# Tables' complex product formed by three real products, with the tables stored by quads of channels

## The chip, the cores and the metric

The kernel runs on one core of one Trainium2 chip. The metric is the device time of one execution in microseconds (us). The core has four engines that do work here: PE (TensorE, matmuls; PEld is its weight load), DVE (VectorE), ACT (ScalarE) and POOL (GpSimd); SP is the engine whose queue issues most of the DMAs. Each engine runs its own instructions strictly in the order in which they were written, and waits at an instruction until what it needs (data, or a buffer to come free) is there.

## The reference

Two branches work on one input x (2048 x 512) and are mixed by a gate:

```python
g = _sigmoid((x * gate_w).sum(-1, keepdims=True))
a = _A_ref(x, ...)      # a long convolution per channel
b = _B_ref(x, ...)      # linear attention with 32 heads
return g * a + (1 - g) * b
```

The change lies in branch A. For each of the 512 channels d it needs a convolution kernel over 2048 time steps l, the real part of a sum over 128 states n of complex exponentials:

```python
logdA = dt * A
P = jnp.exp(logdA[:, :, None] * l[None, None, :])
K = jnp.einsum("dn,dnl,dn->dl", Cc, P, dB).real
```

K is then convolved with the input through a Fourier transform, and a skip term is added.

## The kernel before, in words

**How K is built.** The time index is split in three: l = 512a + 64b + r, with a in 0..3, b in 0..7 and 64 values of r. exp(logdA * l) is then the product of a factor that depends on a (it takes Cc and dB in as well; table Ctab, complex), one that depends on b (table Dtab, complex) and one that depends on r (R, complex, cos and sin rows times a real exponential). States n lie on the 128 partitions; the sum over n is the matmul's contraction. The complex product Ctab x Dtab gives the stationary operand A: 4 x 8 = 32 columns for each channel and each part, and `kgen_chunk` (L168) multiplies it with R into the PSUM tile kps.

**Units.** The 512 channels are done in 16 units of 32. For each unit `plan_conv` writes, in this order by name: A1, A2, A3 (DVE, the product of the tables, L1113 and L1124), Rh and Rl (DVE, L1131 and L1135), kps (PE, L179), KD (its eviction from PSUM, on ACT but for the last), then the transform of two units together (psA, XA, psB, XK, t, psz, Zr, and a turn through DRAM, Zd and ZT, or on DVE). There is one buffer for A, two for R.

**The product before.** Ctab is stored as three planes o = 0, 1, 2 (minus one part, the other part, plus the first part), each of 4 x 256 channels for each half of the channels. Dtab is two planes of 8 x 512. A1 multiplies planes 0 and 1 of Ctab with plane 0 of Dtab, A2 planes 1 and 2 with plane 1; each is one DVE instruction that writes 2048 elements. What is left is the sum of both halves. A string of 16 digits, FOURS, says for each unit who adds: where it is 0 (units 2, 8, 14 and 15) a third DVE instruction A3 (L1124) adds the two halves and PE has two terms (64 matmuls); where it is 1 (the other 12 units) there is no A3, and PE adds in PSUM, with four terms (128 matmuls).

**How the tables are made.** `prepare` makes them, once for each half h of the channels, in steps named p_... on ACT and DVE, between the key stage of branch B and the first unit. ACT makes magnitudes (p_d, Exp into Dtab; p_ce into pmag) and sines and cosines (p_sn into the tile trg, which has one buffer that serves Ctab, then Dtab, then the other half). DVE multiplies: p_pr, p_px and p_cn for Ctab (L393/L394, L433, L440), p_dd and p_de for Dtab (L394, L449).

**What sets the order.** Nothing is scheduled at run time. All steps are nodes of a plan, and the long string ORDER lists the order in which they are written; the string SIDES says for some evictions whether ACT or DVE does them. Waits are derived from which instruction reads and writes which bytes, and from the rings of buffers. PSUM tiles come from rings of two or three; the steps argC (PE, args<-statC, L1035, whose result ACT turns into the sines cs) of the first four units use the same ring `ps` of two buffers as the last steps of the input's transform, psBu, whose evictions (xst, L145 on ACT, L147 on DVE) stand in the queues around the table steps. The sums of branch B's key stage (vp, its eviction vb, vr on DVE at L777, kvp on PE at L785) end at the same place.

Of the kernel before, what the change touches and what calls it, by code (L numbers as in the profile page):

```python
# [194 lines left out]
def prepare(P, nc, g, evict, psum):  # L195
# [227 lines left out]
    for h in range(2):  # L423
# [7 lines left out]
        V("p_pr", lambda h=h, hs=hs: tt(C[h][:, 2], mag()[:, :, hs], F.sc[:, 0], ALU.mult), r="s0 t7 t8", w=f"C{h}")  # L431
        V("p_pr", lambda h=h, hs=hs: tt(C[h][:, 1], mag()[:, :, hs], F.sc[:, 1], ALU.mult), r="s1 t7 t8", w=f"Ci{h}")
        V("p_cn", lambda h=h: nc.vector.tensor_scalar(out=C[h][:, 0], in0=C[h][:, 2], scalar1=-1.0, scalar2=None, op0=ALU.mult), r=f"C{h}", w=f"Cn{h}")  # L433

        def by(o, k, i, h=h, hs=hs):
            tt(o.rearrange("p k a c -> p (k a) c"), C[h][:, i:i + 2].rearrange("p k a c -> p (k a) c"), F.xy[:, k, hs].unsqueeze(1).to_broadcast([128, 8, 256]), ALU.mult)
        V("p_px", lambda by=by: by(F.P[:], 0, 1), r=f"t3 C{h} Ci{h}", w="t5 t6")
        V("p_px", lambda by=by: by(F.Q[:], 1, 0), r=f"t3 Cn{h} Ci{h}", w="t0 t1")
        V("p_px", lambda h=h: tt(C[h][:, 0:2], F.P[:], F.Q[:], ALU.add), r="t0 t1 t5 t6", w=f"Cn{h} Ci{h}")
        V("p_cn", lambda h=h: nc.vector.tensor_scalar(out=C[h][:, 2], in0=C[h][:, 0], scalar1=-1.0, scalar2=None, op0=ALU.mult), r=f"Cn{h}", w=f"C{h}")  # L440
# [631 lines left out]
def plan_conv(P, nc, g, psum, r):  # L1072
# [27 lines left out]
    def kgen(units, XA, new, split=False):  # L1100
        K = Bag()
        K.done, kps, nu = [], [], len(units)
        for cc, U in enumerate(units):
# [4 lines left out]
            d0 = 32 * U

            def half(k, c=c, d0=d0, U=U):  # L1110
                cf = g.C[U // 8][:, k:k + 2, :, d0 % 256:d0 % 256 + 32].rearrange("p o a (q l) -> p (o a) q l", l=4)
# [1 line left out]
                nc.vector.tensor_tensor(out=c.A[:, :, 64 * k:64 * k + 64, :].rearrange("p q (x b) l -> p x b q l", b=8),  # L1113
                                        in0=cf.unsqueeze(2).to_broadcast([128, 8, 8, 8, 4]), in1=df.unsqueeze(1).to_broadcast([128, 8, 8, 8, 4]), op=ALU.mult)
# [523 lines left out]
```

## Time and profile before

| what | before |
|---|---|
| median of three runs | 253.44 us (252.9, 253.44, 254.3) |
| span of the profiled execution | 252.7 us |
| PE, PEld busy | 196.8 us (78%), 132.5 us (52%) |
| DVE busy | 231.5 us (92%) |
| ACT busy | 220.4 us (87%) |
| POOL busy | 20.5 us (8%) |
| mean granted TensorE clock | 0.942 |
| DMA moved | 34.60 MB |

The span is the time from the first to the last instruction of the profiled execution, and the page has no other time of that execution; the median lies 0.74 us above it. Times within the trace are counted from the span's start. In a row of a timeline stand the start, the duration, the engine, the line, the operation, what it writes and reads, and in square brackets how long the engine sat idle before it and what ended that. Where a row has a count, its duration spans from the start of the first to the end of the last.

### The profile page before, as it was taken

The numbers are of one execution on the slowest core, as the hardware profiler recorded it, in microseconds if no ns is written. First come the engines' busy times: TensorE is split into PE (matmuls) and PEld (weight loads), VectorE is DVE, ScalarE is ACT, GpSimd is POOL, SyncE is SP. The second block draws the span as 40 slices with busy tenths as digits, with TensorE's granted clock in tenths as the row PEclk, the third lists the DMA queues.
The fourth block names the chain that finished last, engine by engine and source line by source line (L and its number), as shares of the span: only waits on it lengthen the run. The fifth ranks groups of instructions, "written<-read, shape, count | busy, mean of one in ns | idle before, by whom it ended". The sixth has DMA issues, their size and how long they took to land.

```text
span 252.7 us, 9846 instructions
## 1 busy us (share of the span) xinstructions
PE 196.8 (78%) x4386; PEld 132.5 (52%) x4386; DVE 231.5 (92%) x313; ACT 220.4 (87%) x305; POOL 20.5 (8%) x36
## 2 busy tenths in 40 slices
PE   0378899999977489799577866889879778988980
PEld 0268556566654353254344634575648455777550
DVE  7789999998799998899999999999999989998971
ACT  6897878999999998999999999999999899963640
POOL 5680000000000000000000000000000000020331
PEclk9999999999997658999968999999999999999995
DMA  6899220030472359700540356942966779899326
GB/s 196 139 193 223 60 49 4 3 109 21 127 228 62 113 143 260 232 11 10 145 126 3 107 132 172 299 134 44 249 131 181 211 183 236 193 245 287 67 42 107
DMA packets 54251, 34.60 MB, mean 137 GB/s; under 512 B 34401, under 2 KB 49921, under 8 KB 53825
## 3 DMA queue, kind: packets, MB, share of 16 engines
q1 hardware_dynamic: 53664, 32.73, 52.1%
q0 software_dynamic: 544, 1.25, 2.3%
q8 instruction: 34, 0.56, 0.9%
q14 instruction: 9, 0.07, 0.1%
...
## 4 chain that ended last, share of the span: by engine, by line
PE 31%; DVE 26%; ACT 24%; DMA 8%; issue 7%; SPq 1%; ACTq 0%; POOLq 0%; POOL 0%; DVEq 0%
ACT cs L68 7%; PE pk L720 6%; PE vp L768 5%; DVE A L1113 3%; DVE R L1135 3%; DMA ZT<-Zd 3%; DMA Zd<-Zr 3%; PE psz L1274 3%; DVE R L1131 3%; ACT Zr L145 3%; DMA ax<-apd 2%; PE psA L602 2%; ACT L65 2%; ACT xst L145 2%; PE psB L627 2%
## 5 line engine op out<-in xcount | busy, mean ns | idle before, releaser
L1113 DVE TENSOR_TENSOR A<-Ctab,Dtab 128x2048 bf16<-128x2048 bf16 x32 | 39.0, 1220 | 0.0
L68 ACT ACTIVATE cs<-args 128x1024 bf16<-128x1024 f32 x32 | 30.9, 1056 | 0.7 <-PE args L1035 0.7
L179 PE MATMUL kps<-R,A 128*32 128x64 bf16 x1792 | 19.3, 200 | 7.2 <-ACT XA L145 1.9
L1389 POOL DMA_DIRECT2D out_dram<-xT x10 | 6.4, 650 | 216.8 <-ACT Ctab L145 206.7
L179 PEld LDWEIGHTS <-A 128*32 128x32 bf16 x1792 | 17.8, 116 | 10.7 <-issue 6.0
L1131 DVE TENSOR_TENSOR R<-E,cs 128x2048 bf16<-128x2048 bf16 x16 | 19.5, 1220 | 0.6 <-ACT E L68 0.6
L1135 DVE TENSOR_TENSOR R<-E,cs 128x2048 bf16<-128x2048 bf16 x16 | 19.5, 1219 | 0.0
L1274 PE MATMUL psz<-t,TI 128*128 128x512 bf16 x64 | 16.8, 379 | 2.6 <-issue 1.3
L768 PE MATMUL vp<-WW,xT 128*128 128x512 bf16 x64 | 18.5, 425 | 0.0
L145 ACT CAST XK<-psB 128x1024 bf16<-128x1024 f32 (+1 forms) x16 | 15.8, 1016 | 2.1 <-PE psB L192 1.6
L68 ACT ACTIVATE E<-args 128x1024 bf16<-128x1024 f32 x16 | 16.8, 1050 | 0.8 <-DVE R L1135 0.8
L145 ACT CAST Zr<-psz 128x1024 bf16<-128x1024 f32 (+1 forms) x15 | 14.5, 973 | 3.4 <-PE psz L1274 2.3
L68 ACT ACTIVATE Ek<-pk 128x512 bf16<-128x512 f32 x32 | 16.5, 607 | 1.1 <-PE pk L720 1.1
L854 PE MATMUL pq<-xT,Wqp 128*128 128x512 bf16 x64 | 16.7, 395 | 0.7 <-ACT Eq L68 0.7
L1246 DVE TENSOR_TENSOR t<-XUX,XK 128x2048 bf16<-128x2048 bf16 x14 | 17.0, 1219 | 0.1
L145 ACT CAST XA<-psA 128x1024 bf16<-128x1024 f32 (+1 forms) x15 | 14.4, 976 | 2.8 <-PE psA L186 2.8
L68 ACT ACTIVATE Eq<-pq 128x512 bf16<-128x512 f32 (+1 forms) x28 | 16.7, 721 | 0.1
L627 PE MATMUL psB<-XAu,TB 64*128 64x128 bf16 x256 | 11.3, 250 | 5.6 <-ACT xst L145 4.5
L720 PE MATMUL pk<-WW,xT 128*128 128x512 bf16 x64 | 15.0, 380 | 0.0
L627 PEld LDWEIGHTS <-TB 64*128 64x128 bf16 x256 | 9.5, 110 | 8.5 <-issue 8.3
...
L186 PE MATMUL psA<-W,KD 128*64 128x128 bf16 x256 | 10.0, 221 | 3.1 <-ACT XK L145 1.4
(211 smaller groups left out, 503.3 us busy)
## 6 DMA issues: line engine op xcount, KB each, us to landing
XUX<-XUd SPq DMA_DIRECT2D x32, 256.0 KB, 4.7
...
ax<-apd SPq DMA_DIRECT2D x16, 256.0 KB, 5.2
Zd<-Zr SPq DMA_DIRECT2D x12, 256.0 KB, 3.4
ZT<-Zd SPq DMA_DIRECT2D x12, 256.0 KB, 5.8
...
XUd<-xst SPq DMA_DIRECT2D x8, 256.0 KB, 4.0
...
```

The costliest lines, as they stand in the source:

```text
L65: return self.nc.scalar.preload_act_table_set(name)
L68: return self.nc.scalar.activation(**kw)
L145: self.nc.scalar.copy(out=o, in_=i)
L179: nc.tensor.matmul(kps[32 * dj:32 * dj + 32, g4, e, :], lhsT=A[:, d // 4, 32 * ka:32 * ka + 32, d % 4], rhs=R[:, kr, d, :], start=(i == 0) ...
L627: nc.tensor.matmul(box.ps[:, c2, sl, :], lhsT=fc.TB[rows, b0:b0 + 2].rearrange("p a b -> p (a b)"), rhs=X.t[rows, k, r0 + sl].rearrange("p ...
L720: nc.tensor.matmul(box.ps[:], lhsT=xT[:, st, kt, :], rhs=g.WW[:, kt, :], start=(kt == 0), stop=(kt == 3))
L768: nc.tensor.matmul(box.ps[:], lhsT=xT[:, st, kt, :], rhs=g.WW[:, 4 + kt, :], start=(kt == 0), stop=(kt == 3))
L1113: nc.vector.tensor_tensor(out=c.A[:, :, 64 * k:64 * k + 64, :].rearrange("p q (x b) l -> p x b q l", b=8), in0=cf.unsqueeze(2).to_broadcas ...
L1131: nc.vector.tensor_tensor(out=c.R[:, :, :, 32:64], in0=t.E[:, 1].unsqueeze(1).to_broadcast([128, 2, 32, 32]), in1=t.cs[:], op=ALU.mult)
L1135: nc.vector.tensor_tensor(out=c.R[:, :, :, 0:32], in0=t.E[:, 0].unsqueeze(1).to_broadcast([128, 2, 32, 32]), in1=t.cs[:, ::-1, :, ::-1], o ...
L1246: nc.vector.tensor_tensor(out=box.t, in0=Ls[r0 // ns].X[:], in1=box.XK[:].unsqueeze(1).to_broadcast([128, 2, 1024]), op=ALU.mult)
L1274: nc.tensor.matmul(box.pz[:, hb, :], lhsT=fc.TIp[:, k].rearrange("p h a t -> p (h a t)"), rhs=box.t[:, k, 512 * hb:512 * hb + 512], start= ...
```

## The change

The product of two complex numbers is formed from three real products instead of four. With Ctab's number (p, q) and Dtab's (u, v), the tables now hold sums and differences of the parts ahead of time (three planes each), and A holds three products; PE adds them in PSUM with the signs and pairings that are left, as the four terms (1, 0), (1, 1), (0, 1), (2, 0) of (plane of A, part of R). This is so for all 16 units: FOURS, A3 and the two-term form are gone.

- A1 becomes one DVE instruction of 3072 elements (8 quads of channels x 3 planes x 32 columns x 4 channels). A2 and A3 stay in the plan as steps that write nothing, so that the string ORDER still fits; it, SIDES and RINGS are as they were.
- Both tables are stored by quads of four channels: Ctab as (quad, plane, a, channel in the quad), Dtab as (quad, plane, b, channel in the quad). The steps that make them write runs of four elements.
- p_cn has a second form: where one instruction negated a plane, two now write a difference and a sum of planes. p_de has one instruction more, which writes the third plane of Dtab (2048 elements for each half). dd's order of planes is turned.
- Dtab is half as large again (24 KB for each partition, 16 KB before), A is smaller (6 KB, 8 KB before). To make room, the weights wqk lie in Dtab's bytes until the tables are made (p_d then depends on wtp, PE's reading of them), and three of branch B's tiles oT lie in Dtab's bytes of the first units once these are done (`g.reuse`, which depends on unit 7's A1).

```diff
-    FOURS = ("1101111101111100")
...
-def kgen_chunk(nc, kps, A, R, four):
+def kgen_chunk(nc, kps, A, R):
+    terms = [(1, 0), (1, 1), (0, 1), (2, 0)]
...
-            terms = [(k, k) for k in range(2)] if not four else [(0, 0), (2, 0), (1, 1), (3, 1)]
...
+    wtp = [n for n in P.nodes if n.name == "wtp"]
...
-        S("p_d", lambda b=b: act(out=g.D[:, 0, b, :], in_=are(), func=ACT.Exp, scale=64.0 * (b - 3.5)), r="act t2", w=f"D{b}")
+        S("p_d", lambda b=b: act(out=g.D[:, :, 2, b, :], in_=u4(are()), func=ACT.Exp, scale=64.0 * (b - 3.5)), r="act t2", w=f"D{b}", deps=wtp)
...
-        V("p_cn", lambda h=h: nc.vector.tensor_scalar(out=C[h][:, 2], in0=C[h][:, 0], scalar1=-1.0, scalar2=None, op0=ALU.mult), r=f"Cn{h}", w=f"C{h}")
...
+        def cx(cv=cv):
+            tt(cv(2), cv(0), cv(1), ALU.subtract)
+            tt(cv(0), cv(0), cv(1), ALU.add)
+        V("p_cn", cx, r=f"Ci{h}", w=f"C{h} Cn{h}")
...
-        def de(hs=hs):
-            tt(D[:, 0, 4:8, hs], D[:, 0, 4:8, hs], F.sc[:, 1], ALU.mult)
-            tt(D[:, 0, 0:4, hs], D[:, 0, 0:4, hs], F.sc[:, 1, ::-1], ALU.mult)
+        def de(dv=dv, sv=sv, us=us):
+            tt(dv(2, 4), dv(2, 4), sv(1, 1), ALU.mult)
+            tt(dv(2, 0), dv(2, 0), sv(1, -1), ALU.mult)
+            tt(D[:, us, 1], D[:, us, 2], D[:, us, 0], ALU.subtract)
...
-            def a1(c=c, half=half):
-                c.A = g.wk.tile([128, 8, 128, 4], BF16, name="A", tag="A", bufs=g.P.k["A"])
-                half(0)
-
-            def a2(half=half):
-                half(1)
-
-            def a3(c=c):
-                nc.vector.tensor_tensor(out=c.A[:, :, 0:64], in0=c.A[:, :, 0:64], in1=c.A[:, :, 64:128], op=ALU.add)
+            def a1(c=c, U=U):
+                c.A = g.wk.tile([128, 8, 96, 4], BF16, name="A", tag="A", bufs=g.P.k["A"])
+                cf = g.C[U // 8][:, U % 8 * 8:U % 8 * 8 + 8].rearrange("p u o a l -> p (u o a) l")
+                df = g.D[:, 8 * U:8 * U + 8].rearrange("p u o b l -> p (u o) (b l)")
+                nc.vector.tensor_tensor(out=c.A[:].rearrange("p q (o a b) l -> p (q o) a b l", o=3, a=4),
+                                        in0=cf.unsqueeze(2).to_broadcast([128, 96, 8, 4]).rearrange("p (u a) b l -> p u a b l", a=4),
+                                        in1=df.unsqueeze(2).to_broadcast([128, 24, 4, 32]).rearrange("p u a (b l) -> p u a b l", l=4), op=ALU.mult)
             an = [P.add("DVE", "A1", a1, [sh], take=["A"], rw=(Ck + " " + Dk, ""))]
-            an.append(P.add("DVE", "A2", a2, an[-1:]))
-            an.append(P.add("DVE", "A3", (lambda: None) if four else a3, an[-1:]))
+            an.append(P.add("DVE", "A2", lambda: None, an[-1:]))
+            an.append(P.add("DVE", "A3", lambda: None, an[-1:]))
...
-        g.D = persist.tile([128, 2, 8, 512], BF16, name="Dtab")
+        g.D = persist.tile([128, 128, 3, 8, 4], BF16, name="Dtab")
...
-        g.wqk = g.up.tile([128, 4, 1024], BF16, name="wqk")
+        g.wqk = g.DX[:, 0:4096].rearrange("p (k c) -> p k c", k=4)
```

Three places show how the rows of the queues stand before and after. The first is DVE at the end of the table steps of the second half of the channels (Ctab_75, with Dtab; ppx and ppy are the two products that Ctab is the sum of), up to the eviction xst of the input's transform. Before:

```order
L449 TENSOR_SCALAR trg<-trg 128x1024 [waits DVE_49]
L394 TENSOR_TENSOR Dtab<-Dtab,trg 128x4x256 [waits DVE_49]
L394 TENSOR_TENSOR Ctab_75<-ppx,ppy 128x2048
L394 TENSOR_TENSOR Dtab<-Dtab,trg 128x4x256 [waits DVE_49,Activation_49]
L394 TENSOR_TENSOR Dtab<-Dtab,trg 128x4x256
L440 TENSOR_SCALAR Ctab_75<-Ctab_75 128x1024 [waits DVE_49]
L147 CAST xst<-psB 128x2x4x4x32 [waits DMAHW4_49,DMAHW3_49,DMAHW7_49,DMAHW0_49,PE_49]
L147 CAST vb<-vp 128x512
L777 TENSOR_TENSOR vr<-vb,vr 128x2x512 [waits DVE_49]
```

And after:

```order
L466 TENSOR_SCALAR trg<-trg 128x1024 [waits DVE_49]
L393 TENSOR_TENSOR Dtab<-Dtab,trg 128x4x64x4 [waits DVE_49]
L393 TENSOR_TENSOR Ctab_75<-ppx,ppy 128x8x64x4
L393 TENSOR_TENSOR Dtab<-Dtab,trg 128x4x64x4 [waits Activation_49]
L393 TENSOR_TENSOR Dtab<-Dtab,trg 128x4x64x4 [waits DVE_49]
L393 TENSOR_TENSOR Dtab<-Dtab 128x64x32 [waits DVE_49]
L393 TENSOR_TENSOR Ctab_75<-Ctab_75 128x4x64x4
L393 TENSOR_TENSOR Ctab_75<-Ctab_75 128x4x64x4 [waits DVE_49]
L146 CAST xst<-psB 128x2x4x4x32 [waits DMAHW4_49,DMAHW3_49,DMAHW7_49,DMAHW0_49,PE_49]
L146 CAST vb<-vp 128x512
L795 TENSOR_TENSOR vr<-vb,vr 128x2x512 [waits DVE_49]
```

One instruction of 2048 elements has come in for Dtab; in Ctab's place the negation of 1024 elements has become a difference and a sum of 1024 each; and the parts of Dtab wait for each other, since their bytes now interleave. What follows, xst, vb and vr, is the same and in the same order.

The second place is PE a little later: args of the second unit, between a vp and the first kvp (of a group of 32). Before:

```order
L768 MATMUL vp<-WW,xT 128x512
L1035 LDWEIGHTS statC
L1035 MATMUL args<-selE,statC 128x512 [waits DVE_49]
L1035 LDWEIGHTS statC
L1035 MATMUL args<-selE,statC 128x512
L785 LDWEIGHTS Ek
L785 MATMUL kvp<-vr,Ek 32x34 [waits DVE_49]
```

And after:

```order
L786 MATMUL vp<-WW,xT 128x512
L1055 LDWEIGHTS statC
L1055 MATMUL args<-selE,statC 128x512 [waits DVE_49]
L1055 LDWEIGHTS statC
L1055 MATMUL args<-selE,statC 128x512
L803 LDWEIGHTS Ek
L803 MATMUL kvp<-vr,Ek 32x34 [waits DVE_49]
```

Nothing moved here. The wait of args on DVE is for the PSUM buffer that xst empties, that of kvp for vr.

The third place is DVE in the units, around the third unit (unit 2, the first one that had an A3). Before:

```order
L1113 TENSOR_TENSOR A<-Ctab_74,Dtab 128x64x8x4 [waits PE_49]
L1131 TENSOR_TENSOR R<-E,cs 128x64x32
L1113 TENSOR_TENSOR A<-Ctab_74,Dtab 128x64x8x4
L1065 TENSOR_TENSOR E<-E,Gtab 128x1024
L1124 TENSOR_TENSOR A<-A 128x8x256 [waits DVE_49]
L1135 TENSOR_TENSOR R<-E,cs 128x64x32 [waits DVE_49]
L1113 TENSOR_TENSOR A<-Ctab_74,Dtab 128x64x8x4 [waits DVE_49,PE_49]
```

And after:

```order
L1132 TENSOR_TENSOR A<-Ctab_74,Dtab 128x3072 [waits PE_49]
L1141 TENSOR_TENSOR R<-E,cs 128x64x32
L1085 TENSOR_TENSOR E<-E,Gtab 128x1024
L1145 TENSOR_TENSOR R<-E,cs 128x64x32 [waits DVE_49]
L1132 TENSOR_TENSOR A<-Ctab_74,Dtab 128x3072 [waits PE_49]
```

The whole product of a unit now stands where its first half stood, and the second half and the addition are gone from between the others.

More of the change, by code (lines that the diff above doesn't have):

```diff
@@ L430, in prepare, with cv, c2, by @@
         trig4("p_fc", fill_c, "t4")
[L431 to L440, printed above, removed]
+        def cv(o, h=h):
+            return C[h][:, :, o].rearrange("p u a l -> p a u l")
+        def c2(o, h=h):
+            return C[h][:, :, o:o + 2].rearrange("p u o a l -> p (o a) u l")
+        w4 = lambda a: a.rearrange("p a (u l) -> p a u l", l=4)
+        V("p_pr", lambda hs=hs, cv=cv: tt(cv(2), w4(mag()[:, :, hs]), w4(F.sc[:, 0]), ALU.mult), r="s0 t7 t8", w=f"C{h}")
+        V("p_pr", lambda hs=hs, cv=cv: tt(cv(1), w4(mag()[:, :, hs]), w4(F.sc[:, 1]), ALU.mult), r="s1 t7 t8", w=f"Ci{h}")
+        V("p_cn", lambda cv=cv: nc.vector.tensor_scalar(out=cv(0), in0=cv(2), scalar1=-1.0, scalar2=None, op0=ALU.mult), r=f"C{h}", w=f"Cn{h}")
+        ka = lambda t: t[:].rearrange("p k a (u l) -> p (k a) u l", l=4)
+        def by(o, k, i, c2=c2, hs=hs):
+            tt(ka(o), c2(i), u4(F.xy[:, k, hs]).unsqueeze(1).to_broadcast([128, 8, 64, 4]), ALU.mult)
+        V("p_px", lambda by=by: by(F.P, 0, 1), r=f"t3 C{h} Ci{h}", w="t5 t6")
+        V("p_px", lambda by=by: by(F.Q, 1, 0), r=f"t3 Cn{h} Ci{h}", w="t0 t1")
+        V("p_px", lambda c2=c2: tt(c2(0), ka(F.P), ka(F.Q), ALU.add), r="t0 t1 t5 t6", w=f"Cn{h} Ci{h}")
+        def cx(cv=cv):
+            tt(cv(2), cv(0), cv(1), ALU.subtract)
+            tt(cv(0), cv(0), cv(1), ALU.add)
+        V("p_cn", cx, r=f"Ci{h}", w=f"C{h} Cn{h}")
         def fill_d(hs=hs):
@@ L954, in block @@
                 ot.append(evict("oT" + L, oe, [po, wo]))
+                if b == 2 or (b == 1 and ip):
+                    g.reuse.append(ot[-1])
         def out_mm(ps, i, j):
@@ L1077, in plan_conv @@
     Ck = " ".join(f"C{h} Ci{h} Cn{h}" for h in range(2))
-    Dk = "Di " + " ".join(f"D{b}" for b in range(8))
+    Dk = "Di Ds " + " ".join(f"D{b}" for b in range(8))
     T, on, yn, late = {}, [], [], []
@@ L1139, in kgen, with kp @@
             rn = P.add("DVE", "Rl", rl, [rn, t.nE[1]], drop=["E", "cs"])
-            def kp(c=c, cc=cc, four=four):
+            def kp(c=c, cc=cc):
                 if cc == 0:
                     K.ps = psum([128, 2, 4, 2, 64], "kps")
-                kgen_chunk(nc, K.ps[:, cc], c.A, c.R, four)
+                kgen_chunk(nc, K.ps[:, cc], c.A, c.R)
                 c.A = c.R = None
             if U == 7:
-                g.half = an[1]
+                g.half = an[0]
             kps.append(P.add("PE", "kps", kp, an + [rn] + kps, take=([psq, "KD"] if cc == 0 else []), drop=["A", "R"]))
@@ L1417, in plan_conv @@
             transform(XA, done, h // 2, 0, 128, [load(h // 2, p) for p in range(4)], False)
-    for n in yn:
+    for n in yn + g.reuse:
         n.deps.append(g.half)
@@ L1465, in full_kernel @@
         g.CX = [persist.tile([128, 3072], BF16, name=f"Ctab{h}") for h in range(2)]
-        g.C = [c[:].rearrange("p (o a c) -> p o a c", o=3, a=4) for c in g.CX]
-        g.D = persist.tile([128, 2, 8, 512], BF16, name="Dtab")
+        g.C = [c[:].rearrange("p (u o a l) -> p u o a l", o=3, a=4, l=4) for c in g.CX]
+        g.D = persist.tile([128, 128, 3, 8, 4], BF16, name="Dtab")
+        g.DX = g.D[:].rearrange("p u o b l -> p (u o b l)")
         g.G = persist.tile([128, 512, 2], BF16, name="Gtab")
@@ L1492, in full_kernel @@
         g.ld_b = g.up.tile([128, 512], BF16, name="ld")
-        g.wqk = g.up.tile([128, 4, 1024], BF16, name="wqk")
+        g.wqk = g.DX[:, 0:4096].rearrange("p (k c) -> p k c", k=4)
         g.wc = g.up.tile([128, 4, 16], BF16, name="wc")
-        g.icol, g.oT = {}, {}
+        g.icol, g.oT, g.reuse = {}, {}, []
         def load_ld():
@@ L1513, in load_wqk @@
         def load_wqk():
-            nc.sync.dma_start(out=g.wqk[:], in_=B_wqkv[:, 0:1024].rearrange("(kt p) c -> p kt c", p=128))
+            nc.sync.dma_start(out=g.wqk, in_=B_wqkv[:, 0:1024].rearrange("(kt p) c -> p kt c", p=128))
         def load_wv():
@@ L1556, in shift_keys @@
             g.fpool = pool(ctx, "fpool", side="right")
-            for b in (1, 2):
-                g.oT[b] = [g.fpool.tile([128, 4, 256], BF16, name=f"oT{b}{i}", bufs=1)[:] for i in range(2)]
+            d0 = [g.DX[:, 1024 * i:1024 * i + 1024].rearrange("p (m t) -> p m t", m=4) for i in range(3)]
+            g.oT[1] = [g.fpool.tile([128, 4, 256], BF16, name="oT1", bufs=1)[:], d0[0]]
+            g.oT[2] = d0[1:3]
             g.Y = g.CX[0][:, 0:1536].rearrange("p (j q d) -> p j q d", j=4, q=3)
```

19 lines of the change are left out of this document (8 added, 11 removed).

## The prediction

> **What bounds the kernel now.** I read the page's first part, then the busy time by stretches, then the timelines of the engines at the seams, then the chain of waits at the end.
>
> ```profile
> span 252.7 us, 9846 instructions
> PE 196.8 (78%) x4386; PEld 132.5 (52%) x4386; DVE 231.5 (92%) x313; ACT 220.4 (87%) x305; POOL 20.5 (8%) x36
> ```
>
> DVE is the busiest, but a share of the span mixes stages. Here are the stretches that the change touches; columns: stretch, its length, busy time of PE, PEld, DVE, ACT, POOL, then granted clock, DMA share, GB/s.
>
> ```profile
> 70.00:97.60 27.60, 19.64 (x213) 11.96 (x211) 27.06 (x46) 26.59 (x32) 0.00 (x0) 0.69 0.54 154
> 97.60:105.60 8.00, 6.18 (x132) 2.91 (x130) 6.82 (x13) 7.79 (x9) 0.00 (x0) 1.00 0.82 230
> ...
> 105.60:217.00 111.40, 89.17 (x2566) 60.24 (x2564) 109.21 (x116) 108.74 (x144) 0.00 (x0) 0.97 0.56 144
> ...
> 217.00:230.60 13.60, 10.99 (x340) 9.56 (x335) 13.28 (x15) 9.71 (x11) 1.47 (x2) 1.00 0.94 231
> 230.60:243.57 12.97, 12.97 (x180) 8.09 (x180) 10.32 (x13) 6.20 (x10) 2.84 (x5) 1.00 0.39 98
> ```
>
> The tables are finished in the first stretch (DVE idle 0.54 us, ACT 1.01). The units run from 105.6 to 217: DVE idle 2.19 us, ACT idle 2.66. Two engines are full there, and ACT's work is untouched by the change. However little DVE has to do, this stretch can't end earlier than ACT's 108.74 us after ACT enters it. From 217 on ACT has slack; in the last one PE is full.
>
> **The change part by part.** First DVE, which all the large edits touch:
>
> ```profile
> L1113 DVE TENSOR_TENSOR A<-Ctab,Dtab 128x2048 bf16<-128x2048 bf16 x32 | 39.0, 1220 | 0.0
> L1246 DVE TENSOR_TENSOR t<-XUX,XK 128x2048 bf16<-128x2048 bf16 x14 | 17.0, 1219 | 0.1
> L1065 DVE TENSOR_TENSOR E<-E,Gtab 128x1024 bf16<-128x1024 bf16 x16 | 10.9, 685 | 0.0
> L147 DVE CAST XAu<-psA 128x1024 bf16<-128x1024 f32 x8 | 9.6, 1218 | 0.1
> L394 DVE TENSOR_TENSOR Dtab<-Dtab,trg 128x1024 bf16<-128x1024 bf16 x8 | 5.3, 687 | 0.1
> L1124 DVE TENSOR_TENSOR A<-A 128x2048 bf16<-128x2048 bf16 x4 | 4.9, 1219 | 0.0
> L394 DVE TENSOR_TENSOR Ctab<-ppx,ppy 128x2048 bf16<-128x2048 bf16 x2 | 2.4, 1218 | 0.0
> L440 DVE TENSOR_SCALAR Ctab<-Ctab 128x1024 bf16<-128x1024 bf16 x2 | 0.8, 420 | 0.0
> ```
>
> *Units.* A bf16 product of 1024 elements takes 685 ns, of 2048 1220, so 3072 take 685 + 2 x 535 = 1755. Before: 32 x 1.220 + 4 x 1.219 = 43.9 us; after: 16 x 1.755 = 28.1. That removes 15.8 us from DVE, 0.685 for each unit and 1.219 more in units 2, 8, 14 and 15. Today's A already reads and writes runs of four elements with broadcasts, and costs what the plain t costs (1220 against 1219), so I give the new form, and the table steps with their runs of four, the plain price. [...]
>
> *Tables.* For each half, p_cn's 0.420 becomes 2 x 0.685 (+0.95) and Dtab's third plane is one instruction more (+1.22); and the parts of Dtab now wait for one another twice, at 0.1 us each: two neighbours that don't (vr in the next fence) span 1.29, not 2 x 0.685, and that overlap goes. 2 x 2.37 = 4.7, less what DVE idles there and would otherwise lose (0.54 in all, of which I count 0.3): +4.4 us, bounds 3.8 (no new gaps, idle fully used) and 4.7. All of it stands ahead of xst, in a stretch where DVE has no slack. So DVE saves 15.8 late and pays 4.4 early, and the question is who waits in between:
>
> ```profile
> 94.48 0.42 DVE L440 TENSOR_SCALAR Ctab<-Ctab 128x1024 bf16<-128x1024 bf16 x1
> 94.86 1.23 DVE L147 CAST xst<-psB 128x1024 bf16<-128x1024 f32 x1
> 96.72 1.29 DVE L777 TENSOR_TENSOR vr<-vb,vr 128x1024 bf16<-128x1024 bf16 x2
> 97.36 0.39 PE L1035 MATMUL args<-selE,statC 64*128 64x512 bf16 x2
> 97.68 0.82 PE L785 MATMUL kvp<-vr,Ek 128*32 128x34 bf16 x64
> 97.79 5.61 ACT L68 ACTIVATE cs<-args 128x1024 bf16<-128x1024 f32 x6 [0.18 <-PE args L1035]
> 98.44 0.39 PE L1035 MATMUL args<-selE,statC 64*128 64x512 bf16 x2
> 103.41 1.28 ACT L65 ACT_TABLE_LOAD   x1
> 104.71 1.02 ACT L68 ACTIVATE E<-args 128x1024 bf16<-128x1024 f32 x1
> 105.76 1.23 DVE L1131 TENSOR_TENSOR R<-E,cs 128x2048 bf16<-128x2048 bf16 x1 [0.56 <-ACT E L68]
> ```
>
> The second args (97.36) goes into the PSUM buffer that DVE's xst empties (94.86 + 1.23 = 96.09), so its slack is 1.27 us; PE's queue holds kvp and the next args behind it. With xst 4.4 later, args starts near 100.5, and the cs that reads it near 100.9 instead of 97.79: ACT stands still for 3.1 us. The third args stands behind the kvp that needs the second vr (96.72 + 1.29 = 98.01, after: 102.4); before, args started 0.43 after that vr and its cs could have begun at 98.44 + 0.39; after, 102.4 + 0.43 + 0.39 = 103.2 against 97.79 + 2 x 5.61 / 6 = 99.66 for its cs before. So ACT is 3.6 us late from there on: table load, E, and R on DVE, which waits for E. DVE itself reaches R at 105.2 + 4.4 - 0.69 (one unit's A) = 108.9, E is there at 105.73 + 3.6 = 109.3: ACT is the later one. Of the 4.4, 3.6 arrive on the engine that then runs full for 111 us.
>
> *What ACT can win back.* Only its idle time, and of that what DVE or PE cause:
>
> ```profile
> 124.56 1.02 ACT L68 ACTIVATE E<-args 128x1024 bf16<-128x1024 f32 x1 [0.25 <-DVE R L1135]
> 189.95 1.02 ACT L68 ACTIVATE E<-args 128x1024 bf16<-128x1024 f32 x1 [0.53 <-DVE R L1135]
> 199.26 1.01 ACT L145 CAST Zr<-psz 128x1024 bf16<-128x1024 f32 x1 [0.77 <-DMA ax<-apd]
> 206.12 1.01 ACT L145 CAST XK<-psB 128x1024 bf16<-128x1024 f32 x1 [0.33 <-PE psB L192]
> 217.12 1.01 ACT L145 CAST Zr<-psz 128x1024 bf16<-128x1024 f32 x1 [0.34 <-DMA Zd<-Zr]
> ```
>
> The two waits for R go (0.78): by 124 DVE has won back 3 x 0.69 + 1.22 = 3.3 us of its 4.4, and is then ahead of an ACT that is 3.6 late. Of the other 1.88 (of 2.66) I give half, 0.94, since an earlier A and R let PE start kps sooner. 3.6 - 1.7 = **+1.9 us** at 217; bounds +0.9 (all idle gone) and +3.6 (none).
>
> *PE.*
>
> ```profile
> 108.91 1.26 PE L179 MATMUL kps<-R,A 128*32 128x64 bf16 x128
> 123.39 0.73 PE L179 MATMUL kps<-R,A 128*32 128x64 bf16 x64 [1.28 <-DVE A L1124]
> ```
>
> Four units go from 64 to 128 matmuls: 4 x 0.53 = 2.1 us, in front of which PE waited for A3 that is gone (1.28 in the row); PE is idle 22 of 111 us there. I count nothing, and up to +0.5 where the row behind is needed by ACT at once.
>
> *The end.*
>
> ```profile
> 212.65 4.37 DMA Zd<-Zr
> ...
> 222.26 8.19 DMA ZT<-Zd
> ...
> 226.56 1.22 DVE L1124 TENSOR_TENSOR A<-A 128x2048 bf16<-128x2048 bf16 x1
> 228.92 0.73 PE L179 MATMUL kps<-R,A 128*32 128x64 bf16 x64
> 230.59 0.64 PE L1368 MATMUL psy<-ZT,TJ 128*64 128x128 bf16 x16 [0.94 <-DMA ZT<-Zd]
> ...
> Zd<-Zr SPq DMA_DIRECT2D x12, 256.0 KB, 3.4
> ZT<-Zd SPq DMA_DIRECT2D x12, 256.0 KB, 5.8
> ```
>
> DVE is full from 217 to 230.6 and loses 2 x 1.90 = 3.8 us of work about here (units 14 and 15), so kps ends well before 229.65. But psy waited 0.94 us beyond it for ZT, a read from DRAM behind ACT's Zr. That chain starts on ACT at 212 and has nothing of the change in it; behind it PE is full to 243.57. So the end moves as ACT does.
>
> *At no cost:* p_d's wait for wtp (wtp stands in PE's queue ahead of the transposes that p_d's input comes from); wqk and oT in Dtab's bytes (same DMAs and evictions, no new wait in ACT's queue); the later write of xst to DRAM and the XUX loads behind it on SP's queue (their first reader is the first transform's t, several units on).
>
> **Sum.** Profiled execution: 252.7 + 1.9 = 254.6. The median stands 0.74 above its span: 253.44 + 1.9 = **255.3 us**. The case's own range: +0.9 to +3.6 plus 0.5 of PE, less or more 0.1: 254.3 to 257.4.
>
> **The rivals.**
>
> *The end gets faster (faster).* ACT wins back all its idle time (+0.9 left), and ZT and the Zd ahead of it fall from 8.19 and 4.37 to their medians, 5.8 and 3.4, because an earlier DVE frees XUX buffers earlier and those loads no longer run beside ZT: -3.4, together -2.4, **251.0**. It decides if these two DMAs lose more than 1.9 together. For it: DMA share 0.94 in that stretch. Against: t's other input comes from ACT, so the loads move with ACT.
>
> *The delay is absorbed (no change).* About half of that relief, or table steps whose waits hide: **253.4**.
>
> *DVE is the bound throughout (much faster).* Then 4.4 - 15.8 = -11.4, **242**. The busy row speaks for it, ACT's 108.74 of 111.40 against. [...]
>
> [...]
>
> **How the numbers follow.** Forecast 0.58; faster end 0.17; absorbed 0.13; DVE-bound 0.06; slow forms 0.06. About 0.5% (1.27 us) is what a measurement of this kernel can tell from no change: under 252.2 is faster, over 254.7 slower. The forecast puts 0.50 in slower and 0.08 in same; the faster end 0.11 in faster and 0.06 in same; absorbed is same; the last two are faster and slower. Faster 0.17, same 0.27, slower 0.56. The range takes the forecast's, absorbed, and the upper part of the faster end: 251.8 to 257.4; DVE-bound, slow forms and the rest (0.2) are outside.
>
> **What would show it.** Right: A at 1.75 us x16; the last table step before xst 4 us later; an ACT wait of about 3 us for args before the second cs; ACT's busy time as before while DVE's falls by 11 and its idle time shows up as waits for ACT; R's first row near 109.4; ZT's landing 1 to 3 us later. Wrong: no such ACT wait, or ACT idle well over 3 us between E's first row and the Zr ahead of ZT (then something new waits), or psy released by another than ZT.

## The result, and the profile after

| | before | after |
|---|---|---|
| median | 253.44 us (5 runs, 252.5 to 254.5) | 269.66 us (5 runs, 266.7 to 270.3) |
| ratio | | 1.060, 95% interval 1.053 to 1.067: slower |
| span of the profiled execution | 252.7 us | 264.9 us |

The prediction was 255.3 us, range 251.8 to 257.4: the sign was right, the size was not. The profiled execution after is the quickest of its five (266.68 us). The first part of its page:

```profile
span 264.9 us, 10337 instructions
PE 198.5 (75%) x4642; PEld 134.3 (51%) x4642; DVE 225.0 (85%) x297; ACT 220.3 (83%) x305; POOL 20.6 (8%) x36
```

No engine works noticeably longer than it did, but for PE's 1.7 us (1.8 in PEld); DVE works 6.5 us less (the prediction had 11). The mean granted clock is nearly the same, 0.939 against 0.942. So the 12.2 us of span are waiting, and the question is who waits for what. First the same rows of the timeline, at the end of the table steps, that the prediction worked with:

```profile
101.40 1.22 DVE L146 CAST xst<-psB 128x1024 bf16<-128x1024 f32 x1
102.67 0.61 PE L1055 MATMUL args<-selE,statC 64*128 64x512 bf16 x2 [3.67 <-DVE xst L146]
103.31 1.94 ACT L68 ACTIVATE cs<-args 128x1024 bf16<-128x1024 f32 x2 [4.16 <-PE args L1055]
110.78 1.02 ACT L68 ACTIVATE E<-args 128x1024 bf16<-128x1024 f32 x1
111.83 1.23 DVE L1141 TENSOR_TENSOR R<-E,cs 128x2048 bf16<-128x2048 bf16 x1 [0.51 <-ACT E L68]
```

The chain is the predicted one: xst late, args waits for its PSUM buffer, ACT stands still for it. But xst is 6.5 us late, not 4.4, and R's first row 6.1 us, not 3.6. Now what is new: PE's rows in units 6 and 7, and ACT behind them (`Dtab<-ops` is the eviction into a tile oT that now lies in Dtab's bytes).

```profile
165.45 0.28 PE L853 MATMUL bps<-wo 128*128 128x128 bf16 x2
167.50 0.29 PE L853 MATMUL bps<-wo 128*128 128x128 bf16 x2 [1.78 <-issue]
168.94 1.09 PE L178 MATMUL kps<-R,A 128*32 128x64 bf16 x108
172.60 0.36 PE L178 MATMUL kps<-R,A 128*32 128x64 bf16 x20 [2.57 <-issue]
173.54 0.59 ACT L144 CAST Dtab<-ops 128x512 bf16<-128x512 f32 x1 [2.56 <-PE ops L962]
```

In the trace of before the same kps (unit 7) stands in one piece:

```profile
160.40 1.42 PE L179 MATMUL kps<-R,A 128*32 128x64 bf16 x128
```

PE stops for 2.57 us after the 108th of 128 matmuls of one unit. Within a unit there is nothing to wait for: A and R are there, the PSUM buffer is taken. "issue" means that nothing the profile shows released it. The view of waits sums these up for PE (us in all, times, longest), after:

```profile
PE kps L178 <- issue: 7.8, 5, 2.6
PE bps L853 <- issue: 1.8, 1, 1.8
```

And the same view of before:

```profile
PE kps L179 <- issue: 1.3, 2, 1.0
```

**Where the delay builds up.** ACT runs the same 305 instructions in the same order in every kernel here, so each can be compared with itself. The table gives how many us later than in before (first row: its start there) six of them start, in the kernel after and in the experiments that follow:

| | E, unit 0 | zs | ops evicted | E | Zr | XA, last | span |
|---|---|---|---|---|---|---|---|
| before, us | 104.71 | 125.48 | 162.93 | 189.95 | 217.12 | 233.28 | 252.7 |
| after | 6.1 | 6.9 | 10.6 | 11.1 | 9.8 | 12.2 | 264.9 |
| before, four terms | -0.4 | 1.4 | 6.8 | 7.7 | 6.7 | 10.5 | 263.2 |
| before, DVE + 6.1 us | 5.0 | 5.6 | 5.3 | 5.1 | 4.3 | 3.5 | 256.2 |
| before, PE shifted by 128 | 1.2 | 1.2 | 5.6 | 9.1 | 12.0 | 13.1 | 266.7 |
| after, two terms in four units | 5.5 | 5.0 | 5.2 | 5.0 | 4.1 | 4.7 | 258.0 |
| after, late planes | 0.1 | 4.3 | 10.7 | 11.0 | 9.4 | 12.3 | 265.0 |
| both of these | 0.0 | 2.1 | 1.8 | 2.1 | 0.8 | 0.4 | 253.2 |
| late in pieces, four sums | -0.5 | 0.6 | 1.1 | 0.9 | -0.3 | -1.0 | 251.8 |

After: 6.1 us are lost before the units, and instead of giving 1.7 back there, ACT loses some 4.5 more by 163 us and 1 to 2 at the end.

### The profile page after: what moved, and what is told of

It is laid out like the page before. It is cut to its first block, busy times and chain, and to the rows that moved or that the text cites. A ratio compares the mean times of both kernels' runs of the same rounds, so it can differ in the third digit from the quotient of the medians.

```text
span 264.9 us, 10337 instructions
## 1 busy us (share of the span) xinstructions
PE 198.5 (75%) x4642; PEld 134.3 (51%) x4642; DVE 225.0 (85%) x297; ACT 220.3 (83%) x305; POOL 20.6 (8%) x36
## 4 chain that ended last, share of the span: by engine, by line
PE 38%; ACT 31%; DVE 16%; issue 7%; SPq 3%; DMA 3%; ACTq 0%; POOLq 0%; POOL 0%; DVEq 0%
PE pk L738 5%; ACT cs L68 5%; ACT Eq L68 4%; PE vp L786 4%; PE kps L178 3%; PE psy L853 3%; PE psz L1284 3%; ACT E L68 3%; ACT XA L144 3%; DVE Ctab L393 2%; DVE Dtab L393 2%; ACT XK L144 2%; DMA XUX<-XUd 2%; ACT L65 2%; ACT Zr L144 2%
## 5 line engine op out<-in xcount | busy, mean ns | idle before, releaser
L1132 DVE TENSOR_TENSOR A<-Ctab,Dtab 128x3072 bf16<-128x3072 bf16 x16 | 28.1, 1756 | 9.5 <-PE kps L178 9.4
L178 PE MATMUL kps<-R,A 128*32 128x64 bf16 x2048 | 21.6, 198 | 11.9 <-issue 7.8
L178 PEld LDWEIGHTS <-A 128*32 128x32 bf16 x2048 | 19.8, 116 | 15.5 <-issue 13.2
L786 PE MATMUL vp<-WW,xT 128*128 128x512 bf16 x64 | 17.6, 410 | 0.0
L645 PE MATMUL psB<-XAu,TB 64*128 64x128 bf16 x256 | 10.7, 240 | 7.4 <-ACT xst L144 6.2
L645 PEld LDWEIGHTS <-TB 64*128 64x128 bf16 x256 | 8.9, 105 | 10.3 <-issue 10.2
L1055 PE MATMUL args<-selE,statC 64*128 64x512 bf16 x32 | 7.8, 463 | 7.2 <-DVE xst L146 3.7
```

What stands on the lines that cost most here:

```text
L178: nc.tensor.matmul(kps[32 * dj:32 * dj + 32, g4, e, :], lhsT=A[:, d // 4, 32 * ka:32 * ka + 32, d % 4], rhs=R[:, kr, d, :], start=(i == 0) ...
L645: nc.tensor.matmul(box.ps[:, c2, sl, :], lhsT=fc.TB[rows, b0:b0 + 2].rearrange("p a b -> p (a b)"), rhs=X.t[rows, k, r0 + sl].rearrange("p ...
L786: nc.tensor.matmul(box.ps[:], lhsT=xT[:, st, kt, :], rhs=g.WW[:, 4 + kt, :], start=(kt == 0), stop=(kt == 3))
L1132: nc.vector.tensor_tensor(out=c.A[:].rearrange("p q (o a b) l -> p (q o) a b l", o=3, a=4), in0=cf.unsqueeze(2).to_broadcast([128, 96, 8, ...
```

## The theories

**PE runs out of instructions.** The page counts the packets of the queue that brings instructions (packets, MB, share). After:

```profile
q8 instruction: 36, 0.59, 1.0%
```

Before:

```profile
q8 instruction: 34, 0.56, 0.9%
```

0.59 MB in 36 packets are 16 KB each. By the pages PE has 4642 matmuls after and 4386 before, each with a weight load: 9284 and 8772 instructions. The 512 more come with two packets more, so a packet brings 256 instructions, of 64 bytes each. The DMA records of both traces give each packet as 16384 bytes. Numbered in the order in which they were written, kps of unit 7 begins at PE's instruction 5081 and stops after 216 of its 256, at 5296 = 20 x 256 + 176; kps of unit 3, which begins at 3605, stops after 156, at 3760 = 14 x 256 + 176. The pauses stand at one place in 256. All nine pauses "issue" of over 0.5 us in this trace stand there to within four instructions, and each ends 2.2 to 2.8 us after such a packet has started. The three of before (1.0 to 1.3 us) stand at the same place. And the packet that ends the long one can be seen, in the DMA view of the stretch from 170.1 to 171.3 us:

```profile
q1 hardware_dynamic: 377, 0.36, 92.4%
q8 instruction: 1, 0.02, 5.8%
```

The one packet starts at 170.12, when PE has just stopped, among 377 of data; PE goes on at 172.60. By this theory the change hurts since four units take 256 instructions instead of 128: each kps is then a run of 256 that PE does in 1.26 us, less than the 2.2 to 2.8 us from a packet's start to PE's going on, and all later instructions fall elsewhere on the fetches.

**The prologue**, as predicted but larger: 6 us on DVE ahead of xst.

**The one A buffer.** A new wait, DVE's A for kps (9.4 us in 7 times), could hold up R behind it, as A1 stands early and is one long instruction now.

## Experiments

Ratios are to the kernel before on the same chip, with their 95% interval.

**PE's instructions of after in the kernel before.** Tables, A1, A2 and DVE's order are those of before.

```diff
-    FOURS = ("1101111101111100")
+    FOURS = ("1111111111111111")
```

> The kernel before with four terms in all 16 units: units 2, 8, 14 and 15 lose their A3 (4.9 us of DVE) and PE gets 512 instructions more, so that PE's stream of instructions is, one for one, that of the kernel after; tables, A1, A2 and the rest are as before. PE theory (in the kernel after PE runs out of instructions inside dense runs of matmuls, and whether it does depends on how its instructions fall on the fetches of 256): slower than before by 2 to 5 us, 255.5 to 258.5, with the row kps <- issue at over 4 us in all where before it was 1.3, and pauses of over 1 us inside kps or bps of units 2 to 6. Buffer theory (the new loss in the units is DVE's single A1 that waits for the one A buffer and holds R up): A is as before here, so no loss; 251.5 to 253.5, kps <- issue near 1.3. Both: R's first row at 105.8, as before.

262.2 us, ratio 1.034 (1.023 to 1.045): more than expected. R's first row is at 105.39. PE's pauses are where after has them, at the 78th matmul of unit 3 and the 108th of unit 7:

```profile
131.08 0.82 PE L179 MATMUL kps<-R,A 128*32 128x64 bf16 x50 [2.94 <-issue]
...
168.39 0.36 PE L179 MATMUL kps<-R,A 128*32 128x64 bf16 x20 [2.30 <-issue]
```

DVE had 4.9 us less to do and the kernel got 8 us slower. The A buffer can't be the cause: A is as before here.

**Only the prologue's delay.** Five sums of 2048 elements on DVE, read by nobody, in the steps p_cn of the kernel before:

```diff
-        V("p_cn", lambda h=h: nc.vector.tensor_scalar(out=C[h][:, 2], ...), r=f"Cn{h}", w=f"C{h}")
+        def cn2(h=h):
+            nc.vector.tensor_scalar(out=C[h][:, 2], ...)
+            for _ in range(2 + h):
+                tt(F.P[:], F.P[:], F.Q[:], ALU.add)
+        V("p_cn", cn2, r=f"Cn{h} t0 t1", w=f"C{h} t5 t6")
```

> The kernel before with five sums of 2048 elements (ppx + ppy into ppx, read by nobody) on DVE at the end of Ctab's steps, two in the first half and three in the second: 5 x 1.22 = 6.1 us, as much as the table steps of the kernel after cost more. Nothing else is changed, PE's instructions are those of before. Prologue theory: R's first row at 111 to 112 instead of 105.76, and since ACT has little idle time to give, 4.4 to 6 us slower: 257.8 to 259.5. The prediction's sum (ACT wins back 1.7 or more): 256 to 257.8. If PE's fetches alone make the whole difference: under 255.5.

258.9 us, ratio 1.024 (1.012 to 1.035).

```profile
100.34 1.22 DVE L147 CAST xst<-psB 128x1024 bf16<-128x1024 f32 x1
...
104.64 3.77 ACT L68 ACTIVATE cs<-args 128x1024 bf16<-128x1024 f32 x4 [4.38 <-PE args L1040]
...
110.96 1.22 DVE L1136 TENSOR_TENSOR R<-E,cs 128x2048 bf16<-128x2048 bf16 x1
```

xst, args and ACT hand the delay on as the prediction has it. What ACT wins back is another matter. In the table above the 5.0 us at E shrink to 4.3 at Zr, where the prediction counts 1.7 won back, and to 3.5 at the last XA; but the profiled execution is the quickest of the four (257.96 us), and by the ratio 6.0 of the 6.1 us put in are lost. A is that of before here, so the run says nothing on the two waits for R that the prediction let go.

**The place of the instructions alone.** 64 matmuls of 8 columns into a PSUM tile that is overwritten afterwards, once in after and once in before:

```diff
                 box.ps = bank("vp")
+                for _ in range(64 if st == 15 else 0):
+                    nc.tensor.matmul(box.ps[0:32, 0:8], lhsT=g.ident[:, 0:32], rhs=g.ident[:, 0:8], start=True, stop=True, ...)
```

> The kernel after with 64 matmuls of 8 columns more on PE (128 instructions with their weight loads, half a fetch, written into the PSUM tile of the last value projection before that is computed) at 97 us, where PE then waits 3.7 us for xst. They cost nothing by themselves, but all later instructions fall otherwise on the fetches. PE theory: R's first row as in the kernel after (111.8), and from there on the pauses lie elsewhere: the time changes by over 1.5 us, by more chance down than up, 263 to 268, and the pauses inside kps of unit 3, bps and kps at 165 to 173 are gone or moved. Buffer theory and prologue theory: no change, 268.5 to 270.5.

> The kernel before with nothing but 64 matmuls of 8 columns more on PE (128 instructions with their weight loads, written into the PSUM tile of the last value projection ahead of its computation, 0.7 us of PE). PE theory: pauses can only stand at one place in every 256 instructions; with that place moved by 128, four-term units meet it that did not before, so the kernel is slower by 1.5 to 6 us: 255.3 to 260, and R's first row is later by less than 1 us. If instruction fetches do not matter: 253.5 to 254.7.

After with them: ratio 1.073 (1.053 to 1.092), not the gain that I expected: without them it is 1.060 (1.053 to 1.067), and since the intervals overlap, this run shows no change of the time either way. The pauses did move: its trace has none of over 0.5 us between 136 and 191 us, and a new one of 2.99 us at 191.88. Before with them: 267.5 us, ratio 1.048 (1.038 to 1.059), a loss of 12 to 14 us and far more than expected, from 64 matmuls that have nothing to do with the change. R's first row is 1.2 us late (106.98), the rest comes later. kps of unit 7 now begins at 4953 + 128 = 5081, as in after, and stops at the same 108th matmul, with the tables and the A of before:

```profile
167.08 0.46 PE L179 MATMUL kps<-R,A 128*32 128x64 bf16 x20 [2.57 <-issue]
...
168.54 0.59 ACT L145 CAST oT<-ops 128x512 bf16<-128x512 f32 x1 [3.08 <-PE ops L946]
...
190.32 0.29 PE L880 MATMUL zs<-Eq,SSw 128*32 128x128 bf16 x8 [3.62 <-issue]
```

**PE's list of before in the kernel after.** Two of four terms in units 2, 8, 14 and 15, whose kernels K so lack half of their products; DVE's work stays.

```diff
-    terms = [(1, 0), (1, 1), (0, 1), (2, 0)]
+    terms = [(1, 0), (1, 1), (0, 1), (2, 0)][0:2 if two else 4]
```

> The kernel after, but PE computes only the first two of its four terms in units 2, 8, 14 and 15 (those units' kernels K then lack half of their products); DVE's work, the tables and all else are those of the kernel after. PE's instructions are then again as many as in the kernel before (8774) and fall on the fetches as there. PE theory: the pauses at units 2 to 6 and at the end shrink to what before has, and the kernel is 5 to 9 us faster than the kernel after (269.66): 260.5 to 264.5; what is left against before is the prologue's 5 to 6 us and a little more. Prologue theory alone, or the one A buffer: 4 x 0.53 us of PE less, 267.5 to 269.5.

259.9 us, ratio 1.024 (1.017 to 1.031): 256 matmuls less, which are 4 x 0.53 = 2.1 us of PE, take away 9 us. The pauses are gone; the view of PE's waits has left:

```profile
PE psz L1284 <- issue: 0.9, 1, 0.9
PE kps L178 <- issue: 0.5, 2, 0.3
```

What is left of the loss is what the prologue costs alone (1.024, above). With A's saving in place, ACT's 5.5 us at E are 4.1 at Zr in the table, so 1.4 are won back there in this trace; by the ratio 6.0 us are still lost at the end. The clock is no rival for these 9 us: the profiled execution has a mean granted clock of 0.924, below the 0.939 of after. In round numbers the ratios add up: 3.4% for PE's list and 2.4% for the prologue are 5.8%, and the change costs 6.0%.

**The prologue's part taken out of after.** The third plane and Ctab's sum and difference move behind xst, into steps of the plan that stand empty there:

```diff
-        V("p_cn", cx, ...)
+        g.cx.append(cx)
+        V("p_cn", lambda: None, ...)
...
-            tt(D[:, us, 1], D[:, us, 2], D[:, us, 0], ALU.subtract)
+        def ds(us=us):
+            tt(D[:, us, 1], D[:, us, 2], D[:, us, 0], ALU.subtract)
+        g.ds.append(ds)
...
+            a = {0: (pre, a1), 2: (a1, lambda: g.ds[1]()), 4: (a1, lambda: g.cx[1]())}.get(U, (a1, lambda: None))
```

Here `pre` does both for the first half. Then the same together with the two terms of the last run:

> The kernel after with the added table steps moved out of the stretch ahead of xst: Dtab's third plane and Ctab's sum and difference (2 x (1.23 + 1.62) = 5.7 us of DVE) are written for the first half of the channels just ahead of unit 0's A, which comes after zrow, and for the second half behind the A of units 2 and 4. PE's instructions are those of the kernel after. Prologue theory: xst at 95.5 to 96.5 instead of 101.4, R's first row at 107 to 108.5 instead of 111.8, time 3 to 4.5 us less than the kernel after: 265 to 266.7. If PE's pauses make up most of the loss and depend on timing: between 262 and 270, with the gain at R lost again by 175. Buffer theory: no gain, since DVE stays the one that waits for kps in the units.

> Both cures at once on the kernel after: two terms in units 2, 8, 14 and 15 (half of those units' products left out) and the added table steps moved behind xst. If PE's fetches and the prologue are the whole loss: 253 to 258, within 2% of before. If a third cost is left (the one A buffer, the longer A instruction): over 259.

Late planes alone: 267.4 us, ratio 1.052 (1.038 to 1.066); xst is at 95.39 and R at 107.73. The delay at E is gone (0.1 us), yet at 163 us it is 10.7 as in after: PE's pauses are there (2.3 and 2.3 us in the same bps and kps), the moved steps now stand on DVE among the first units (at zs, ahead of these pauses, ACT is 4.3 late again), and in this execution the granted clock fell for a while, as the windows from 130 to 150 us show (clock after POOL's busy time):

```profile
130.00:150.00 20.00, 15.14 (x420) 10.17 (x421) 17.02 (x18) 18.29 (x26) 0.00 (x0) 0.70 0.17 51
```

In the kernel after, about the same work, six microseconds later:

```profile
136.00:156.00 20.00, 15.29 (x440) 9.66 (x427) 19.11 (x22) 19.93 (x29) 0.00 (x0) 0.91 0.24 62
```

How much of the 10.7 us is the clock, how much the pauses and how much the moved steps can't be told from one trace. With both changes: 254.6 us, ratio 1.007 (1.002 to 1.012). That leaves little room for a third cost, such as the A buffer.

**Single forms, and PE with nothing to wait for.**

> A kernel that computes nothing of the reference (out is a copy of u): it times single forms. DVE: products of 1024 bf16 elements by runs of four, whose quads step by 32, 64, 80, 96, 128, 192 and 256 bytes on the writing side, the reading side and both; the plain form takes 0.685 us. If the step of 96 bytes is what made Ctab's steps slower: 0.78 to 0.80 at 96, 0.685 to 0.69 at 192; if the runs of 8 bytes were the cause: 0.78 at all of them. PE: eight four-term kps in a row (2048 instructions) with all inputs ready and no DMA beside them, then eight more while 4 MB of loads and stores run. PE theory: the first eight take 20 us or more instead of 8 x 1.26 = 10, with a pause of about 1.3 us in every 256 instructions, which ends 2.2 to 2.9 us after an instruction fetch began; the second eight take longer still, 3.5 us or more for each 256. Rival: 10 to 11 us and no pauses.

The groups of DVE, products of 1024 elements by runs of four; b, d and f are quads that step by 64, 96 and 192 bytes, q is written, rd is computed from q; the last is the plain form:

```profile
L59 DVE TENSOR_TENSOR qb<-mag,trig 128x1024 bf16<-128x1024 bf16 x2 | 1.4, 692 | 0.1
L59 DVE TENSOR_TENSOR qd<-mag,trig 128x1024 bf16<-128x1024 bf16 x2 | 1.6, 798 | 0.1
L59 DVE TENSOR_TENSOR rdd<-qd,trig 128x1024 bf16<-128x1024 bf16 x2 | 1.6, 791 | 0.1
L59 DVE TENSOR_TENSOR qf<-mag,trig 128x1024 bf16<-128x1024 bf16 x2 | 1.4, 693 | 0.1
L59 DVE TENSOR_TENSOR mag<-mag,trig 128x1024 bf16<-128x1024 bf16 x3 | 2.1, 690 | 0.1
```

At 32, 64, 80, 128, 192 and 256 bytes all forms take 688 to 696 ns, at 96 bytes 791 to 798. Ctab's quads step by 96 bytes, Dtab's by 192. PE's timeline, first without and then (last three rows) beside the DMAs:

```profile
12.67 3.16 PE L48 MATMUL kps<-R,A 128*32 128x64 bf16 x223 [12.67 <-DVE R L64]
17.30 1.26 PE L48 MATMUL kps<-R,A 128*32 128x64 bf16 x128 [1.47 <-issue]
20.76 1.90 PE L48 MATMUL kps<-R,A 128*32 128x64 bf16 x128 [2.19 <-issue]
24.21 1.91 PE L48 MATMUL kps<-R,A 128*32 128x64 bf16 x128 [1.55 <-issue]
...
85.10 1.90 PE L48 MATMUL kps<-R,B 128*32 128x64 bf16 x128 [1.93 <-issue]
91.03 1.90 PE L48 MATMUL kps<-R,B 128*32 128x64 bf16 x128 [4.02 <-issue]
96.12 1.90 PE L48 MATMUL kps<-R,B 128*32 128x64 bf16 x128 [3.19 <-issue]
```

After 223 matmuls, which are 446 instructions, PE stops at every 256th, and goes on every 3.45 us (17.30, 20.76, 24.21; one of the six intervals is 3.73), whether the 128 matmuls in between took 1.26 or 1.90 us (the mean granted clock of this run is 0.585). Beside 4 MB of loads and stores it goes on after 5.93 and 5.09 us, and then after 3.45 to 4.01 us. So this dense run got 256 instructions in 3.45 us at best, where PE did them in 1.26 to 1.90 us. In the kernel after, the packet that follows the long pause starts at 173.74, 1.14 us after PE has gone on at 172.60; with the 2.2 to 2.8 us from a packet's start to PE's going on that makes 3.3 to 3.9 us, about what the dense run shows (an estimate).

**Choosing the place.** A shift by 40 instructions instead of 128, on top of late planes (the same few lines as above with 20 matmuls). And a try to bring all of PE's list in after back to the places of before, with bare weight loads as filler:

```diff
+                def pad():
+                    for _ in range(128):
+                        nc.tensor.ldweights(g.ident[:, 0:32])
+                if U in (2, 9, 15):
+                    pad()
...
+                if U == 15:
+                    pad()
```

> The kernel after with the added table steps behind xst (as in the run with late planes, 267.38) and 20 small matmuls (40 instructions) more on PE ahead of the units. By adding up, over the trace of that run, how much less than 3.8 us lies between the places 256 instructions apart, a shift by 40 is the best of all: 7.4 instead of 10.3 us of pauses. PE theory: 263 to 266.5, while a shift by 128 in the other kernels cost time. If only chance decides: 266 to 270.

> The kernel after, output unchanged, with 4 x 128 weight loads of 32 columns more on PE that nothing uses (ahead of kps of units 2, 9 and 15, and behind that of unit 15). With the 128 instructions that units 2, 8, 14 and 15 have more than before, that makes 256 each time, so that all other instructions fall on the fetches of 256 as in the kernel before, and kps of units 2 and 8 are cut in the middle. PE theory: although PE does more (1.2 us each), the pauses in the units are nearly gone and the time falls from 269.66 to 259 to 263.5. If it is the number of PE's instructions that costs, and not where they fall: slower than the kernel after, 270 to 275.

> As the one before, and the added table steps moved out of the prologue in pieces: ahead of unit 0's A only what units 0 and 1 need (a quarter), the rest of the first half of the channels beside units 1 and 2, the second half beside units 4 and 6. Output unchanged. PE and prologue theories together: R's first row at 106 to 107 and 252.5 to 256.5, as before within 1%; under 252.2 it would be faster than both kernels. If the weight loads collide with PE's work in the units: 257 to 262.

Shift by 40: 265.4 us, ratio 1.046 (1.041 to 1.052) against 1.052 (1.038 to 1.066): as expected in sign, but the intervals overlap. The 3.8 us that I counted with were an estimate; the dense run has intervals of 3.45 to 5.93 us. The 7.4 us of pauses that were expected are not there: in its profiled execution, the slowest of the four, PE's idle time with "issue" adds up to 14.4 us, so this choice of a place did not work as it was worked out. The filler failed: 278.0 us (1.098, 1.093 to 1.103), and with the table steps late in pieces 274.5 (1.080, 1.075 to 1.086). Its rows in the latter say why:

```profile
129.93 0.37 ACT L68 ACTIVATE zs<-zs 128x256 f32<-128x256 f32 x1 [4.08 <-PE zs L902]
...
235.68 1.64 PEld L1164 LDWEIGHTS <-ident 128*32 128x32 bf16 x85
...
242.81 3.49 PEld L1164 LDWEIGHTS <-ident 128*32 128x32 bf16 x128
246.31 1.06 PE L1395 MATMUL psy<-ZT,TJ 128*64 128x128 bf16 x16 [3.43 <-issue]
```

The 128 bare weight loads at 242.81 took 3.49 us, 27 ns each; the 85 at 235.68 took 1.64 us, 19 ns each. I had counted 1.2 us for 128. Those at 242.81 and the kps beside them are 384 instructions in a row. ACT's delay jumps at these places and only there: 4.8 us at the first, 4.1 at the second, 10.5 at the last; between them it stays level or falls (4.5 to 4.4, 8.5 to 6.8). That fits the theory, but as a cure it was badly made, and no run here shows a filler that pays.

**A version with fewer instructions.** The middle product can be added to the two others on DVE, where PE then has two terms; done in units 2, 8, 14 and 15 this makes PE's list as long as that of before, row for row. The table steps are late in pieces: a quarter of the first half ahead of unit 0's A, the rest beside units 1, 2, 4 and 6.

```diff
-    terms = [(1, 0), (1, 1), (0, 1), (2, 0)]
+    terms = [(2, 0), (0, 1)] if two else [(1, 0), (1, 1), (0, 1), (2, 0)]
...
+            def a3(c=c):
+                v = c.A[:].rearrange("p q (o x) l -> p q o (x l)", o=3)
+                nc.vector.tensor_tensor(out=v[:, :, 0:3:2], in0=v[:, :, 0:3:2], in1=v[:, :, 1:2].to_broadcast([128, 8, 2, 128]), op=ALU.add)
```

> Three products as in the kernel after, output unchanged, with both cures that the runs so far point to. PE: in units 2, 8, 14 and 15 DVE adds the middle product to the two others (1.22 us, in the place of the A3 of before), so that PE has two terms there, and its stream is again as long as that of before, row for row (8774). DVE: the added table steps are moved behind xst in pieces, a quarter of the first half ahead of unit 0's A, the rest beside units 1, 2, 4 and 6. PE and prologue theories: R's first row at 105.5 to 106.5, no pause of over 1.7 us in the units, and 251.5 to 254.5; DVE's busy time near 230 and yet little or no gain on before, since ACT is full from 105 to 217 us. Under 252.2: faster than both kernels. Over 256: a third cost of the three products is left.

255.2 us, ratio 1.006 (1.003 to 1.009): 14 us better than after, no better than before. In the profiled execution R starts at 105.45, and the stretch from 105.6 to 217 us reads (columns as in the prediction):

```profile
105.60:217.00 111.40, 87.25 (x2559) 60.06 (x2562) 106.72 (x109) 108.41 (x144) 0.00 (x0) 0.98 0.54 142
```

DVE is 4.7 us idle here, in before 2.2; ACT is as full as it was (108.4 of 111.4). DVE's gain is small in this version, 228.3 us busy in all against 231.5. With two terms and late planes it is larger, 7.4 us idle in the same stretch (104.00 busy, ACT 108.00), and that kernel is no faster either (1.007): DVE's gain has nowhere to go. Where the last 0.6% is lost is open; this profiled execution (253.5 us) is one of the quickest and does not show it.

## Why the prediction was wrong, point by point

- *Units.* Right: 16 A rows of 1756 ns, 28.1 us, 15.8 less than before.

```profile
L1132 DVE TENSOR_TENSOR A<-Ctab,Dtab 128x3072 bf16<-128x3072 bf16 x16 | 28.1, 1756 | 9.5 <-PE kps L178 9.4
L393 DVE TENSOR_TENSOR Ctab<-pmag,trg 128x1024 bf16<-128x1024 bf16 x4 | 3.2, 789 | 0.0
L393 DVE TENSOR_TENSOR Ctab<-ppx,ppy 128x2048 bf16<-128x2048 bf16 x2 | 2.9, 1426 | 0.0
L393 DVE TENSOR_TENSOR Ctab<-Ctab 128x1024 bf16<-128x1024 bf16 x4 | 3.2, 794 | 0.1
L393 DVE TENSOR_TENSOR ppx<-Ctab,pt 128x2048 bf16<-128x2048 bf16 x2 | 2.8, 1422 | 0.0
L393 DVE TENSOR_TENSOR Dtab<-Dtab,trg 128x1024 bf16<-128x1024 bf16 x8 | 5.3, 687 | 0.1
L393 DVE TENSOR_TENSOR Dtab<-Dtab 128x2048 bf16<-128x2048 bf16 x2 | 2.5, 1226 | 0.1
```

- *Tables.* Mis-sized: +4.4 was counted. xst came 6.5 us later, of which 0.4 was there ahead of the first table step. The steps on Ctab take 789 to 794 ns for 1024 elements and 1422 to 1426 for 2048, where I had counted 685 and 1220; those on Dtab kept 687 and 1226. The single forms tell why: it is the step of 96 bytes, not the runs. All forms with these runs of 8 bytes took the plain time at six other steps (688 to 696 ns, the plain form 690). The A row from which I took the plain price (1220 ns for 2048 elements) has these runs too, but is another form.
- *Who waits.* The mechanism was right, with sizes of 4.16 us instead of 3.1 for the first wait and 6.1 instead of 3.6 at R, as DVE was later.
- *What ACT can win back.* Not borne out: the prediction takes 1.7 us off by Zr. The traces have 0.7 there with the prologue's delay alone and 1.4 with A's saving as well, but both kernels are 6.0 us slower by their ratios (1.024). So the sum of +1.9 us for the prologue measured about 6.0. In the kernel after ACT's idle time grew.
- *PE.* This is the step that failed: "I count nothing, and up to +0.5". The 512 instructions more were priced by their run time (2.1 us). They cost 8 us alone (1.034), as they move every later instruction to another place in the blocks of 256 and make four more runs of 256. This is the larger part of the miss of 14.4 us; the prologue's 6.0 instead of 1.9 us is another 4.1, and the 2 us that remain lie within the intervals.
- *The end.* After kps of unit 15 psy follows in PE's order, not a wait for ZT; kps itself had been interrupted for 1.74 us. This and ACT's idle time were named as signs that something new waits, and so it was.
- *The rivals.* None of them came, slow forms (0.06) among them: A took the 1756 ns that its plain price gives, and of the table steps those on Ctab alone took more than theirs; xst was 6.5 us late in all.

Some of it is not settled. Why one fetch starts 2.6 us after PE has entered a block (at 170.12, just as PE stopped; PE had entered it at 167.50) and the next one 1.1 us after (173.74 and 172.60) is only argued from the DMAs beside it; in the dense run 256 instructions took 5.1 to 5.9 us beside loads and stores, against 3.45 us without. The size of a loss by shifting was not predicted well either: 12 to 14 us for before where 1.5 to 6 were expected.
